# Regrouping the first tiles of a pruned matrix product: tiles 3 to 6 in one group of rows, one transposing load per tile

## The chip, the cores and the metric

The kernel runs on one core of a Trainium2 chip. The metric is the device time of one execution in microseconds (us), the median over several runs. The core has a matrix engine (PE, with its weight loads shown apart as PEld), a vector engine (DVE), a scalar engine (ACT), GpSimd (POOL) and a sync engine (SP). SP and ACT also issue transfers here: each has a queue in which its instructions are taken strictly in order, and the transfers of both run on the same 16 DMA engines.

## The reference

```python
B, S, D = 16, 512, 1024
wg = w.reshape(G, M, D)                       # M = 4 neighbouring rows of w
mag = jnp.abs(wg)
order = jnp.argsort(mag, 1)
thr = jnp.take_along_axis(mag, order[:, M - N:M - N + 1, :], 1)   # N = 2
mask = (mag >= thr).astype(w.dtype)
wp = (wg * mask).reshape(D, D)                # the two largest of four are kept
return jnp.einsum("bsd,df->bsf", x, wp) + b
```

The input x has 8192 rows (tokens) of K = 1024 numbers, w is 1024 by 1024, everything is bfloat16.

## The kernel before

**Tiles.** The 8192 rows are 64 tiles of 128 rows. PE contracts over partitions, so a tile of x must stand in SBUF with K on the partitions: transposed. For most tiles the load itself transposes (`dma_start_transpose`). The kernel takes the two halves of K apart at the start: the "upper" half is K 0 to 511 (`HK` = 512, g = 0), the "lower" half K 512 to 1023 (g = 1).

**The first seven tiles.** Pruning w takes DVE and ACT some 25 us, piece by piece (six pieces; four of the upper half of K with 256 columns each, two of the lower with 512). So that PE can begin early, the upper halves of tiles 0 to 6 (`NPK` = 7) are loaded untransposed (`load_x`), transposed by PE itself (tokens `T`, line 195), copied out by ACT (`C`), and multiplied with each piece as soon as it is pruned (`M`, line 216). Their sums over the upper half are copied to SBUF by ACT (`S`, `U`). Pruned pieces are also spread to another layout, `wp_nat`, by plain transfers (tokens `W`: `W0.0` and `W0.1` for the two column halves of the upper K, `W1.0`, in the parts p on SP and q on ACT, and `W1.1` for the lower K); every spread issues one transfer for each of four blocks of 128 rows of K, and each matmul of line 244 reads one such block.

**Groups.** A transposing load is done for the lower halves of tiles 0 to 5 (`load_low`, tokens `Y`), and `GROUPS` says which rows a tile means there: within a group of n tiles, row n*p + t of the group is row p of its tile t (`tokens`, line 93). Input and output use the same view, so the tiles of a group interleave their rows. Before, the groups are tiles 0 to 2, 3 to 5 and 6 alone. One transposing load takes a whole group of 384 rows, and the weight loads of a tile read every third column of it. Tile 6 (`SOLO`), alone in its group, has its lower half in the transposing load of tiles 7 to 11 (`load_lead`, 5 "lead" tiles): `X0` loads the upper halves of tiles 7 to 11 (640 rows), `X1` the lower halves of 6 to 11 (768 rows).

**Closing.** Tiles 7 to 11 get their upper half on PE (tokens `E` and `A`) while the lower half of w is still being pruned. Then 24 closes follow (line 416), one for each of the tiles 0 to 11 and column half: four matmuls over the lower half of K with `wp_nat`'s last four blocks, and an eviction by DVE that adds the bias or the stored upper sum. Their order is (8,0) (9,0) (10,0) (11,0) (7,0) (6,0) (3,0) (4,0) (5,0), the same nine with column half 1, and then (2,0) (2,1) (0,0) (0,1) (1,0) (1,1). After them come batches of 4 and six times 8 tiles, 16 matmuls a tile, from transposing loads of whole rows (`load_batch`, tile xb, two buffers). `outp` has ten output buffers, `psum_o` six banks.

**Order.** The order on PE, DVE, ACT and SP is written out by hand in the strings of `order` (line 268); SP's is:

```python
        "sp": (
            "W0.0 Z W0.1 X1 W1.0p Y1 Y0 W1.1"
        ),
```

In front of it SP issues part of the loads of w and x and then X0; behind it the first two xb. `Z` loads the last columns of w and the bias. PE's string begins "T5a T3a T4a T6a M5.0t M3.0t". The order of a queue's instructions is also the order in which they wait: what stands behind a waiting instruction waits with it.

Of the kernel before, what the change touches and what calls it, by code (L numbers as in the profile page):

```python
# [10 lines left out]
def kernel(  # L11
# [7 lines left out]
    nc = tc.nc  # L19
    P = 128  # L20
    bf16 = mybir.dt.bfloat16
# [7 lines left out]
    KT = D // P  # L29
# [3 lines left out]
    FH = 512  # L33
    CW = 256
    HK = D // G
    assert G == 2 and Dout == 2 * FH and HK == 512
    xf = x.flatten_outer_dims()
    of = out.flatten_outer_dims()

    NPK = 7  # L40
    LEAD = 5
    STG = 8
    SOLO = 6
    GROUPS = ((0, 3), (3, 6), (6, 7))
    LATE = 6
    sizes = (4, 8, 8, 8, 8, 8, 8)
    batches = []
    t0 = NPK + LEAD
# [5 lines left out]
    const = ctx.enter_context(tc.tile_pool(name="const", bufs=1))  # L54
# [11 lines left out]
    def seq(eng, inst):  # L66
        if eng in tails:
            tc.add_manual_dep(inst.ins, tails[eng].ins.name, NOSYNC, reason="program order")
        tails[eng] = inst
        return inst  # L70

    def pe(i):
        return seq("pe", i)
# [7 lines left out]
    def sp(i):  # L81
        return seq("sp", i)
# [10 lines left out]
    def tokens(dram, t):  # L93
        a, b_ = next(s for s in GROUPS if s[0] <= t < s[1])
        return dram[a * P:b_ * P].rearrange("(p t) k -> p t k", p=P), t - a
# [13 lines left out]
        for t in range(ta, tb):  # L109
            x_sb[t] = xs[:, t - ta, :]  # L110

    xlead = const.tile([P, KT, (LEAD + 1) * P], bf16)

    def load_lead(g):
        t0 = NPK - g
        sp(nc.sync.dma_start_transpose(out=xlead[:, 4 * g:4 * g + 4, (t0 - SOLO) * P:],
                                       in_=xf[t0 * P:(NPK + LEAD) * P, g * HK:(g + 1) * HK]))
        return {t: xlead[:, :, (t - SOLO) * P:(t - SOLO + 1) * P] for t in range(t0, NPK + LEAD)}

    xnat, held = {}, {}  # L120

# [10 lines left out]
    load_w(0, 768, 1024)  # L132
    load_w(1, 0, 512)
    xnat.update(load_lead(0))
    pieces = [(0, 0, 256), (0, 256, 512), (0, 512, 768), (0, 768, 1024), (1, 0, 512), (1, 512, 1024)]

# [95 lines left out]
                                start=(new and m == ms.start), stop=(left[key] == 0),  # L232
                                skip_group_check=True))

    def load_low(u):
        a, b_ = GROUPS[u]
        xlow = const.tile([P, 4, (b_ - a) * P], bf16, name=f"xlow{u}")
        sp(nc.sync.dma_start_transpose(out=xlow[:], in_=xf[a * P:b_ * P, HK:]))
        xq = xlow[:].rearrange("p k (q t) -> p k q t", t=b_ - a)
        return {a + t: xq[:, :, :, t] for t in range(b_ - a)}  # L240

    def nat(xt, ps, c0, c1, k0=0, k1=KT, first=0, last=KT - 1, koff=0):
        for kt in range(k0, k1):
            pe(nc.tensor.matmul(ps, lhsT=xt[:, kt - koff, :], rhs=wp_nat[:, kt, c0:c1],  # L244
                                start=(kt == first), stop=(kt == last)))
# [15 lines left out]
    def stage(key):  # L261
        solo = key[1] == "h"
        q, h, at = (pair_of[key[0]], key[2], int(key[0] != SOLO)) if solo else (key[0], key[1] // 2, key[1] % 2)
        if (q, h) not in staged:
# [21 lines left out]
            "S3b3 S2b3 U7h0 W1.0q U7h1"  # L286
        ),
        "sp": (
            "W0.0 Z W0.1 X1 W1.0p Y1 Y0 W1.1"
        ),  # L290
    }
    written = {"X0"}
    p = {}
# [53 lines left out]
    def emit(eng, tok):  # L347
# [10 lines left out]
        elif tok[0] == "Z":  # L358
            load_w(1, 512, 1024)
            sp(nc.sync.dma_start(bias_sb[:], b.partition_broadcast(P)))  # L360
        elif tok[0] == "X":
            xnat.update(load_lead(int(tok[1:])))
        elif tok[0] == "Y":
            xnat.update(load_low(int(tok[1:])))
        elif tok[0] == "E":
            open_solo(int(tok[1:]))
        elif tok[0] == "U":
            t, h = map(int, tok[1:].split("h"))
            stage((t, "h", h))
        elif tok[0] == "A":  # L370
            open_nat(*map(int, tok[1:].split("h")))
        elif tok[0] == "C":
            copy_xt(int(tok[1:-1]))
        elif tok[0] == "M":
            mm_piece(*map(int, base[1:].split(".")), part[k])
        elif tok[0] == "S":
            stage(tuple(map(int, tok[1:].split("b"))))
        else:
            i = int(base[-1])
            if i not in p:  # L380
                p[i] = Piece(i)
            if eng == "act":
                p[i].abs_act()
            else:
                p[i].do(base[:-1], part[k], half.get(k, slice(0, 2)))
# [42 lines left out]
    def evac(o, ps, c0, c1, add=None):  # L428
        if add is None:
            dve(nc.vector.tensor_tensor(o[:, c0:c1], ps, bias_sb[:, c0:c1], op=Alu.add))  # L430
        else:
            dve(nc.vector.tensor_tensor(o[:, c0:c1].rearrange("p (n c) -> p n c", n=2),  # L432
                                        ps.rearrange("p (n c) -> p n c", n=2), add, op=Alu.add))
# [7 lines left out]
    def store(eng, t, o, c0=0, c1=Dout):  # L441
        issue(eng, rows(t)[:, c0:c1], o[:, c0:c1])
# [4 lines left out]
    def close(t, h):  # L447
        if t not in outs:
            outs[t] = outp.tile([P, Dout], bf16, name="o")
        ps = held.pop((t, h), None)  # L450
        if ps is None:
            ps = psum_o.tile([P, FH], fp32, name="ps")
        nat(xnat[t], ps[:], h * FH, (h + 1) * FH, 4, 8, first=4 if t < STG else 0, koff=4 if t < SOLO else 0)
        add = None
        if t < STG:
            st, at = staged[(pair_of[t], h)], pairs[pair_of[t]].index(t)
            add = st[:, at, :, :] if SOLO in pairs[pair_of[t]] else st[:, :, at, :]
        evac(outs[t], ps[:], h * FH, (h + 1) * FH, add)
        closed[t] = closed.get(t, 0) + 1
        if closed[t] == 2:  # L460
            store("act", t, outs.pop(t))

    for t, h in closes:
        close(t, h)
# [3 lines left out]
    for bi, (tb, nb) in enumerate(batches):  # L468
        if bi:
            load_batch(bi + 1)  # L470
        for j in range(nb):
            t = tb + j
            xt = xnat[t]
            o = outp.tile([P, Dout], bf16, name="o")
            if t == NT - 1:
                for n, (c0, c1) in enumerate(((0, FH), (FH, FH + CW), (FH + CW, Dout - P), (Dout - P, Dout))):
                    ps = psum_o.tile([P, FH], fp32, name="ps")
# [44 lines left out]
```

## Time and profile before

| | us |
|---|---|
| median of 3 runs | 233.0 |
| lowest, highest | 232.53, 233.31 |
| the profiled execution, its own time | 233.15 |
| its span, first to last instruction | 231.3 |
| PE busy | 227.1 (98%) |
| PE weight loads busy | 110.5 (48%) |
| DVE busy | 107.8 (47%) |

The views read below are rows of one profiled execution. A row of a timeline has start, length, engine, line, operation, what it writes and reads, how many instructions are merged, and in brackets the idle time before it and what ended it. SPq and ACTq are the queues' own instructions, such as the issuing of a transfer; a transfer lands some time after its issue. A row of a tile's view has the shortest, median and longest duration in ns, and the first and last start in us.

### The profile page before, as it was taken

The page shows a single profiled execution, that of the slowest core. Times are in us where ns is not written, and L with a number is a line of the kernel's source. Part 1 is how long each engine was busy: PE and PEld are TensorE (multiplying, and loading weights), DVE is VectorE, ACT ScalarE, POOL GpSimd, SP SyncE. Part 2 cuts the span into 40 slices and gives each one's busy share as a digit, 9 for nine tenths or more (in the row PEclk, how much of TensorE's full clock was granted, in tenths as well). Part 3 has the DMA queues.
Part 4 walks back from the last instruction along what each step waited for, and adds up shares of the span by engine and source line. Part 5 has one row for each costly group of instructions (what it writes and reads, how often), then busy time and mean ns, then how long its engine had stood idle before and what let it go on. Part 6 is the DMA issues. An engine that isn't in the chain of part 4 may idle for free.

```text
span 231.3 us, 2831 instructions
## 1 busy us (share of the span) xinstructions
PE 227.1 (98%) x1144; PEld 110.5 (48%) x1144; DVE 107.8 (47%) x196; ACT 14.0 (6%) x27; POOL 17.6 (8%) x15
## 2 busy tenths in 40 slices
PE   8899999999999999999999999999999999999995
PEld 4886444444444444444444444444444444444443
DVE  3999878844324324424424424424423423433434
ACT  3784100000000000000000000000000000000000
POOL 1000199700000000000000000000000000000000
PEclk9999999999999999999999999999999999999999
DMA  6999989998699222991249821796128942122122
GB/s 200 270 206 252 231 176 223 230 296 241 224 197 300 92 94 66 260 263 53 86 116 252 221 91 67 146 254 196 69 91 204 238 148 84 55 91 91 50 89 91
DMA packets 79292, 38.19 MB, mean 165 GB/s; under 512 B 64176, under 2 KB 71728, under 8 KB 79280
## 3 DMA queue, kind: packets, MB, share of 16 engines
q1 hardware_dynamic: 68352, 20.75, 44.3%
q10 hardware_dynamic: 10928, 17.27, 21.4%
q8 instruction: 9, 0.15, 0.3%
q14 instruction: 3, 0.02, 0.1%
HBM read 3.28 MB, written 16.78 MB: 87 GB/s over the span
## 4 chain that ended last, share of the span: by engine, by line
PE 96%; DMA 2%; ACTq 0%; DVE 0%; issue 0%
PE ps L244 88%; PE ps L230 5%; PE tp L244 2%; DMA x<-in_x_dram 2%; ACTq L100 0%; PE ps L200 0%; PE tp L200 0%; DVE o L430 0%
## 5 line engine op out<-in xcount | busy, mean ns | idle before, releaser
L244 PE MATMUL ps<-wp_nat,xb 128*128 128x512 bf16 (+2 forms) x848 | 179.8, 375 | 0.0
L244 PEld LDWEIGHTS <-xb 128*128 128x128 bf16 x848 | 82.4, 98 | 97.5
L430 DVE TENSOR_TENSOR o<-ps,bias_sb 128x512 bf16<-128x512 f32 (+1 forms) x112 | 71.6, 677 | 113.0 <-PE ps L244 112.9
L426 POOL TENSOR_TENSOR st<-st,bias_sb 128x1024 f32<-128x1024 f32 x8 | 16.7, 2125 | 0.0
L244 PE MATMUL ps<-wp_nat,xlead 128*128 128x512 bf16 x64 | 14.8, 379 | 0.0
L244 PEld LDWEIGHTS <-xlead 128*128 128x128 bf16 x88 | 8.6, 98 | 10.2
L230 PE MATMUL ps<-wp,xt 128*128 128x256 bf16 x112 | 12.9, 273 | 0.0
L432 DVE TENSOR_TENSOR o<-ps,st 128x512 bf16<-128x512 f32 x16 | 11.0, 691 | 3.6 <-PE ps L244 2.0
L230 PEld LDWEIGHTS <-xt 128*128 128x128 bf16 x112 | 10.7, 98 | 1.2
L244 PE MATMUL ps<-wp_nat,xlow 128*128 128x512 bf16 x48 | 10.7, 379 | 0.0
L266 ACT COPY st<-ps 128x512 f32<-128x512 f32 x14 | 7.4, 595 | 3.4 <-PE ps L230 3.3
L244 PEld LDWEIGHTS <-xlow 128*128 128x128 bf16 x48 | 5.0, 103 | 5.4
L164 DVE TENSOR_TENSOR mag<-mag,hi 128x256 bf16<-128x256 bf16 (+2 forms) x15 | 6.2, 439 | 0.2
L164 DVE TENSOR_TENSOR wp<-w_sb,mag 128x256 bf16<-128x256 bf16 (+2 forms) x15 | 6.1, 436 | 0.1
L244 PE MATMUL tp<-wp_nat,xlead 128*128 128x512 bf16 x24 | 6.0, 379 | 0.0
L143 PE MATMUL ps<-const-bfloat16-1.0 128*128 128x128 bf16 (+1 forms) x20 | 3.9, 380 | 0.8 <-PEq L506 0.8
L174 DVE TENSOR_SCALAR mag<-w_sb 128x512 uint16<-128x512 uint16 (+2 forms) x5 | 2.3, 477 | 3.5 <-DMA w_sb<-in_w_dram 3.5
L143 PEld LDWEIGHTS <-const-bfloat16-1.0 128*128 128x128 bf16 x20 | 2.1, 135 | 2.4 <-issue 2.4
L164 DVE TENSOR_TENSOR hi<-mag 128x512 bf16<-128x512 bf16 (+2 forms) x7 | 3.2, 459 | 0.1
L164 DVE TENSOR_TENSOR lo<-mag 128x512 bf16<-128x512 bf16 (+1 forms) x6 | 3.1, 509 | 0.0
L200 PEld LDWEIGHTS <-x 128*128 128x128 bf16 x28 | 1.9, 115 | 1.3 <-DMA x<-in_x_dram 1.2
L415 POOL COPY pruned<-wp 128x1 bf16<-128x1 bf16 x1 | 0.2, 187 | 26.8 <-DVE wp L164 26.8
(18 smaller groups left out, 18.1 us busy)
## 6 DMA issues: line engine op xcount, KB each, us to landing
out_dram<-o ACTq DMA_DIRECT2D x58, 256.0 KB, 2.4
wp_nat<-wp SPq DMA_DIRECT2D x14, 128.0 KB, 3.6
out_dram<-o ACTq DMA_DIRECT2D x10, 128.0 KB, 1.7
w_sb<-in_w_dram SPq DMA_DIRECT2D x2, 512.0 KB, 5.6
w_sb<-in_w_dram SPq DMA_DIRECT2D x3, 256.0 KB, 5.4
x<-in_x_dram SPq DMA_DIRECT2D x2, 256.0 KB, 4.5
x<-in_x_dram ACTq DMA_DIRECT2D x2, 128.0 KB, 4.1
bias_sb<-in_b_dram SPq DMA_DIRECT2D x1, 256.0 KB, 4.8
```

The source lines that it names most:

```text
L143: pe(nc.tensor.matmul(warm_ps[:, :rep * P], lhsT=nc.const_aps.tensor(1.0, [P, P], bf16), rhs=nc.const_aps.tensor(1.0, [P, rep * P], bf16), ...
L164: dve(nc.vector.tensor_tensor(out, a, b_, op=op))
L174: dve(nc.vector.tensor_single_scalar(self.mag[:, ms, :].bitcast(u16), self.w[:, ms, :].bitcast(u16), 0x7FFF, op=Alu.bitwise_and))
L200: pe(nc.tensor.transpose(tp[:, m, :], xg[:, m, :], ident[:]))
L230: pe(nc.tensor.matmul(ps[:, c0 + d:c1 + d], lhsT=xpk[t][:, m, :], rhs=wp[:, g, m, c0:c1], start=(new and m == ms.start), stop=(left[key] = ...
L244: pe(nc.tensor.matmul(ps, lhsT=xt[:, kt - koff, :], rhs=wp_nat[:, kt, c0:c1], start=(kt == first), stop=(kt == last)))
L266: act(nc.scalar.copy(staged[(q, h)][:, at, :, :].rearrange("p t c -> p (t c)"), ps_open.pop(key)[:]))
L415: pool(nc.gpsimd.tensor_copy(out=pruned[:], in_=wp[:, 1, 3, Dout - 1:]))
L426: pool(nc.gpsimd.tensor_tensor(st[:], st[:], bias.to_broadcast([P, 2, 2, CW]), op=Alu.add))
L430: dve(nc.vector.tensor_tensor(o[:, c0:c1], ps, bias_sb[:, c0:c1], op=Alu.add))
L432: dve(nc.vector.tensor_tensor(o[:, c0:c1].rearrange("p (n c) -> p n c", n=2), ps.rearrange("p (n c) -> p n c", n=2), add, op=Alu.add))
```

## The change

Tile 6 joins the group of tiles 3 to 5, which has four tiles then, so that row 4p + t of the group is row p of tile 3 + t; tiles 0 to 2 stay as they are. X1 loads tiles 7 to 11 alone, like X0. Each of the tiles 0 to 6 gets a transposing load of its own for its lower half: 128 rows, which lie three rows apart in the first group and four in the second. On SP's queue Y6, Y3, Y4 and Y5 come ahead of W1.1, and Y2, Y0 and Y1 behind it.

```diff
-    GROUPS = ((0, 3), (3, 6), (6, 7))
+    GROUPS = ((0, 3), (3, 7))
...
-    xlead = const.tile([P, KT, (LEAD + 1) * P], bf16)
+    xlead = const.tile([P, KT, LEAD * P], bf16)
 
     def load_lead(g):
-        t0 = NPK - g
-        sp(nc.sync.dma_start_transpose(out=xlead[:, 4 * g:4 * g + 4, (t0 - SOLO) * P:],
-                                       in_=xf[t0 * P:(NPK + LEAD) * P, g * HK:(g + 1) * HK]))
-        return {t: xlead[:, :, (t - SOLO) * P:(t - SOLO + 1) * P] for t in range(t0, NPK + LEAD)}
+        sp(nc.sync.dma_start_transpose(out=xlead[:, 4 * g:4 * g + 4, :],
+                                       in_=xf[NPK * P:(NPK + LEAD) * P, g * HK:(g + 1) * HK]))
+        return {t: xlead[:, :, (t - NPK) * P:(t - NPK + 1) * P] for t in range(NPK, NPK + LEAD)}
...
-    def load_low(u):
-        a, b_ = GROUPS[u]
-        xlow = const.tile([P, 4, (b_ - a) * P], bf16, name=f"xlow{u}")
-        sp(nc.sync.dma_start_transpose(out=xlow[:], in_=xf[a * P:b_ * P, HK:]))
-        xq = xlow[:].rearrange("p k (q t) -> p k q t", t=b_ - a)
-        return {a + t: xq[:, :, :, t] for t in range(b_ - a)}
+    def load_low(t):
+        xlow = const.tile([P, 4, P], bf16, name=f"xlow{t}")
+        xv, n = tokens(xf, t)
+        sp(nc.sync.dma_start_transpose(out=xlow[:], in_=xv[:, n, HK:]))
+        return {t: xlow}
...
-            "W0.0 Z W0.1 X1 W1.0p Y1 Y0 W1.1"
+            "W0.0 Z W0.1 X1 W1.0p Y6 Y3 Y4 Y5 W1.1 Y2 Y0 Y1"
...
-        nat(xnat[t], ps[:], h * FH, (h + 1) * FH, 4, 8, first=4 if t < STG else 0, koff=4 if t < SOLO else 0)
+        nat(xnat[t], ps[:], h * FH, (h + 1) * FH, 4, 8, first=4 if t < STG else 0, koff=4 if t < NPK else 0)
```

## The prediction

> **What bounds the kernel now.** I read the page first, then PE's busy time by stretches, the chain of work that ended last, and the timelines of PE, DVE and SP's queue around the lines that change. The page and the stretches:
>
> ```profile
> PE 227.1 (98%) x1144; PEld 110.5 (48%) x1144; DVE 107.8 (47%) x196; ACT 14.0 (6%) x27; POOL 17.6 (8%) x15
> ...
> PE 96%; DMA 2%; ACTq 0%; DVE 0%; issue 0%
> ```
>
> ```profile
> 6.37:28.34 21.97, 21.97 (x169) 1.00 1.05 236
> 28.34:48.70 20.36, 20.36 (x96) 1.00 1.07 227
> 48.70:228.70 180.00, 179.97 (x850) 1.00 0.57 149
> ```
>
> Columns: stretch, length, PE busy (instructions), granted clock, DMA share, GB/s. From 6.37 us to 228.70 us PE never stops, at full clock. The change removes no matmul, so after 6.37 there is nothing to win. Time can be won only before 6.37, and lost wherever something new makes PE wait. The chain shows what sets 6.37, and PE's timeline the gap (the bracket is idle time before the row):
>
> ```profile
> 1.78 4.54 DMA x<-in_x_dram
> 6.33 0.05 issue
> 6.37 0.41 PE ps L200 x4
> 6.79 1.31 PE ps L230 x12
> ```
>
> ```profile
> 5.36 0.39 PE L200 MATMUL ps<-ident,x 128*128 128x128 bf16 x4
> 6.37 0.41 PE L200 MATMUL ps<-ident,x 128*128 128x128 bf16 x4 [0.63 <-DMA x<-in_x_dram]
> 6.62 1.47 PE L230 MATMUL ps<-wp,xt 128*128 128x256 bf16 x12
> ```
>
> The load issued at 1.78 is the second x load on ACT's queue, load_x(SOLO, SOLO + 1): the upper half of tile 6. T6a waits for it, and the first real matmul (M5.0t) stands behind T6a.
>
> The other limits are SP's queue and, from 19 to 49 us, the DMA engines, whose share is over 1 in the stretches above.
>
> ```profile
> 5.71 5.87 SPq L116 DMA_TRANSPOSE xlead<-in_x_dram  x1
> ...
> 19.80 3.45 SPq L116 DMA_TRANSPOSE xlead<-in_x_dram  x1
> 23.35 1.81 SPq L100 DMA_DIRECT2D wp_nat<-wp  x2
> 25.21 3.83 SPq L238 DMA_TRANSPOSE xlow<-in_x_dram  x2
> ```
>
> ```profile
> 29.13 3.45 SPq L100 DMA_DIRECT2D wp_nat<-wp  x4
> 32.63 4.07 SPq L404 DMA_TRANSPOSE xb<-in_x_dram  x1
> ```
>
> In order: X0; X1; W1.0p; Y1 and Y0; W1.1; the first xb.
>
> **The change, part by part.**
>
> *Tile 6's upper half and the loads beside it.* Same bytes and same 1 KB runs; the rows read for tile 6 lie 8 KB apart, not 2 KB, those of tiles 3 to 5 8 KB, not 6 KB. The trace has 8 KB steps: the first two loads of w take two rows of 512 bytes out of every 8 KB. The first two rows here are those loads; the other two are all five x loads, and the two of ACT's queue.
>
> ```profile
> w_sb<-in_w_dram SPq DMA_DIRECT2D x1, 128.0 KB, 2.8
> ...
> w_sb<-in_w_dram ACTq DMA_DIRECT2D x1, 128.0 KB, 3.0
> ```
>
> ```profile
> DMA to landing us min/median/max: 3.6/4.5/5.2
> ```
>
> ```profile
> DMA to landing us min/median/max: 3.6/4.1/4.5
> ```
>
> With 8 KB steps 128 KB landed in 2.8 and 3.0 us, so the step itself does not look dear. Tile 6's 4.54 is the slower of the two ACT loads, though it is as large as the other. Bounds for tile 6's load: 3.6 (the fastest x load) and 5.2 (the slowest). A faster landing is not all gain, since M5.0t needs the first product of DVE:
>
> ```profile
> 5.97 0.49 DVE L164 TENSOR_TENSOR wp<-w_sb,mag 128x256 bf16<-128x256 bf16 x2
> ```
>
> The first of these two products takes some 0.28 us (284 ns, as the shortest of their kind), so M5.0t cannot start before about 6.25 + 0.05 = 6.30 against 6.62. The gain is at most 0.32 us; the loss at 5.2 us is 0.66. I take 0.2 of gain: the new load moves as much as the ACT load that landed in 3.6, so it is likelier nearer to that one than above 4.54.
>
> *X1 shrinks from 768 rows to 640.* 3.45 us over 768 rows is 4.5 ns a row, so 2.88 us: X1's issue ends at 22.68, not 23.25. W1.0p needs the product that ends at 21.23 + 1.23 = 22.46, so it starts at 22.72, 0.63 earlier:
>
> ```profile
> 21.23 1.23 DVE L164 TENSOR_TENSOR wp<-w_sb,mag 128x2048 bf16<-128x2048 bf16 x1
> ...
> 26.81 1.22 DVE L164 TENSOR_TENSOR wp<-w_sb,mag 128x2048 bf16<-128x2048 bf16 x1
> ```
>
> PE waits for none of it now, so the worth is 0. It is cover: the last spread of W1.0p is issued at 24.4 and lands at 28.1 (the rows below), and the second matmul of the first close needs it at 28.18 + 0.22 = 28.40. The cover grows from 0.3 to about 0.9, less what the front gains.
>
> ```profile
> L100 SPq DMA_DIRECT2D wp_nat<-wp x1: 800/800/800, 24.4 to 24.4; - x1
> ...
> DMA to landing us min/median/max: 3.7/3.7/3.7
> ```
>
> ```profile
> 28.18 2.75 PE L244 MATMUL ps<-wp_nat,xlead 128*128 128x512 bf16 x12
> ```
>
> *Two loads of 384 rows become seven of 128, in two groups.* Price of one, first by the two loads of before:
>
> ```profile
> L244 PEld LDWEIGHTS <-xlow x48: 102/103/104, 33.1 to 48.5; 128*128 128x128 bf16 x48
> ...
> L238 SPq DMA_TRANSPOSE xlow<-in_x_dram x2: 1421/1892/2362, 25.2 to 26.7; - x2
> ...
> DMA to landing us min/median/max: 4.6/5.3/6.0
> ```
>
> A third of each is 0.47 and 0.79 us. X0's 5.87 us over 640 rows (9.2 ns a row, in the crowd of the first loads) would make 1.17. A fixed price per load is bounded below by nothing; above, I let a small load cost all that a large one does, 2.36. Value: a third of 1.89, 0.63, and 0.04 between two, 0.67 each, as the first xb (512 rows of twice the width in 4.07 us, 3.98 ns per row of 512) shows no fixed part: larger loads are not cheaper by the row than 1421 ns over 384 rows (3.7).
>
> W1.0p ends at 22.72 + 1.81 = 24.53; Y6, Y3, Y4 and Y5 take 4 x 0.67 = 2.68 and end at 27.25. W1.1 then waits for its product, 26.81 + 1.22 = 28.03, and starts at 28.09 instead of 29.13: 1.04 earlier. At 1.17 it starts at 24.57 + 4.84 = 29.41, 0.28 later; at 2.36, at 34.17, 5.04 later. Who waits: the first close with the upper columns, whose last matmul needs W1.1's last spread:
>
> ```profile
> L100 SPq DMA_DIRECT2D wp_nat<-wp x1: 603/603/603, 32.0 to 32.0; - x1
> ...
> DMA to landing us min/median/max: 3.1/3.1/3.1
> ```
>
> ```profile
> 35.95 2.75 PE L244 MATMUL ps<-wp_nat,xlead 128*128 128x512 bf16 x12
> ```
>
> It lands at 32.0 + 3.1 = 35.1; PE wants it between 35.95 (if the close waits for all four) and 36.60. So W1.1 may come 0.9 us later for nothing, and comes 1.04 earlier: 0. The lower halves are wanted later still: closes follow each other by 4 x 0.216 = 0.864 us from 28.18, so tiles 6, 3, 4, 5 at 32.5, 33.4, 34.2 and 35.1, tile 2 at 43.7. With 6.0 us from issue to landing Y6 is there at 30.6 and Y5 at 32.6 (34.2 at 1.17 each). None waits.
>
> *W1.1 moves ahead of Y2, Y0, Y1, and these ahead of the first xb.* W1.1's 3.45 end at 31.54, three loads at 0.67 end at 33.6: the first xb starts at 33.6 instead of 32.63, 1.0 later (3.9 at 1.17 each). The first and the second xb before:
>
> ```profile
> L404 SPq DMA_TRANSPOSE xb<-in_x_dram x1: 4072/4072/4072, 32.6 to 32.6; - x1
> ...
> DMA to landing us min/median/max: 6.4/6.4/6.4
> ```
>
> ```profile
> L404 SPq DMA_TRANSPOSE xb<-in_x_dram x1: 15961/15961/15961, 36.7 to 36.7; - x1
> ...
> DMA to landing us min/median/max: 18.0/18.0/18.0
> ```
>
> The first would land 6.4 us after issue at 40.0, at the worst 42.9; tile 12 wants it at 48.7. The second landed at 54.7; 3.9 later is 58.6, and tile 16 wants it at 48.9 + 4 x 3.45 = 62.7. Cost 0 by both bounds. Stores share the DMA engines with it and free DVE's output buffers; DVE waited once:
>
> ```profile
> 48.90 4.48 PE L244 MATMUL ps<-wp_nat,xb 128*128 128x512 bf16 x20
> 49.23 1.29 DVE L432 TENSOR_TENSOR o<-ps,st 128x512 bf16<-128x512 f32 x2 [1.09 <-DMA out_dram<-o]
> ```
>
> Behind that eviction PE has six banks: it stalls only when tile 14 begins, at 48.9 + 2 x 3.45 = 55.8. Stores can be 5 us later than now and cost nothing.
>
> *Weight loads of xlow.* Columns with a step of three become contiguous. The loads took 102 to 104 ns (above), against 97 or 98 from xlead, under matmuls that start 216 ns apart (20 of them in 4.48 us, the last one 379 ns long): 0 either way.
>
> ```profile
> L244 PEld LDWEIGHTS <-xlead x88: 97/98/98, 19.4 to 40.7; 128*128 128x128 bf16 x88
> ```
>
> Sum against the profiled execution's own time, 233.15 (span 231.3, 1.85 around it): 233.15 - 0.2 + 0 + 0 + 0 + 0 = 232.95. It stands 0.15 above the median of 233.0; I forecast 232.9.
>
> The Trainium skill speaks against the split: "DMA: Bandwidth & Descriptors", section "Rules for kernel authors", tells to coalesce many small transfers, as under 64 KB mostly overhead is paid, and to make one at least 1 MiB; its "Latency and other measured facts" has a fixed cost of some 2 us. Paid in turn on the queue, these 2 us would make W1.1 about 3.5 us late and the sum some 236, by that page an estimate. The rows show the fixed part as latency that overlaps: four spreads were issued in 3.45 us though each landed 3 us and more after its issue.
>
> **The rivals.** (1) *Slower: a small transposing load has a fixed price, and W1.1 comes late.* It decides from (29.13 + 0.9 - 24.57) / 4 = 1.37 us for each of the four loads. At 2.36 W1.1 is 5.04 late, less 0.9 to 1.54 of cover: 3.5 to 4.1 of stall, 236.5 to 237; at 1.9 about 235. For it: one 384-row load did take 2.36. Against: the other took 1.42 for the same work, so 2.36 was crowd, not a fixed price. (2) *Slower: tile 6's load lands later*, at 5.2 us, as 8 KB steps over one stretch shared by four tiles: 0.66 more, 233.8; from 0.7 on it can be measured. Against: the w loads above. (3) *Faster: in executions not shown PE stalls at 28.40 or 35.95*, where covers are 0.3 and 0.9, and the change widens both. With the full 0.32 of the front, 232.2. Against: the profiled execution, slower than the median, shows no such stall. (4) *Later xb loads push the stores until DVE and then PE wait*: decides from 5 us, 234. (5) *It wins nothing at all*, tile 6 landing as before: 233.1, within the forecast.
>
> **How the numbers follow.** Forecast, with (5): 0.62. (1) 0.09, (2) 0.14, (3) 0.12, (4) 0.03. A measurement of this kernel tells about 0.3% (0.7 us) from no change. Faster is (3) and the luck of the forecast's lower end: 0.13; slower (1), (2) and (4), less the part of (2) under 0.7: 0.25; same 0.62. The range reaches from (3) to a little above (2): 232.2 to 234.1; the forecast's own is 232.5 to 233.5.
>
> **What would show it.** Right: T6a starts at 6.1 to 6.4 in PE's timeline, PE busy without a gap from there, W1.1's issue at about 28.1, each Y under 0.9 us, the first xb at 33 to 35. Wrong: a wait of PE for DMA at tile 6 longer than 0.63, or for wp_nat near 36 us; or a gain over 0.7 us, for which the trace of before has no place.

## The result and the profile after

| | before | changed |
|---|---|---|
| median of 20 runs, us | 232.94 | 233.35 |
| lowest, highest | 232.53, 233.54 | 232.86, 234.24 |
| the profiled execution, its span | 233.15, 231.3 | 233.39, 231.6 |

The ratio is 1.0017, with a 95% interval of 1.0009 to 1.0025: 0.41 us slower by the medians. That is less than 0.3%, but the 20 runs a side resolve it, and a small gain had been forecast. A few executions of the runs below, at a lower granted clock, took 237 us or more; the ratios and intervals leave them out, the medians do not.

The stretches of PE in the changed kernel, with the columns of before:

```profile
6.37:28.34 21.97, 21.95 (x170) 1.00 1.00 236
28.34:48.70 20.36, 20.36 (x96) 1.00 0.91 198
48.70:228.70 180.00, 180.00 (x850) 1.00 0.61 153
```

In this execution PE is still all but without a gap from its first real matmuls to its end. The whole difference of the two profiles, 0.27 us of span, must lie at the two ends. Start of the PE timeline and the landings of ACT's two x loads, changed kernel:

```profile
5.05 1.04 PE L199 MATMUL tp<-ident,x 128*128 128x128 bf16 x8
5.89 0.75 PE L199 MATMUL ps<-ident,x 128*128 128x128 bf16 x8
6.48 0.69 PE L229 MATMUL ps<-wp,xt 128*128 128x256 bf16 x3
```

```profile
DMA to landing us min/median/max: 3.7/4.1/4.4
```

Tile 6's half lands 0.17 us sooner, at 6.16, and M5.0t starts at 6.48 instead of 6.62. Yet nothing of it is left later: the first eight transposes took 1.04 us against 0.64, the copies of ACT came later, and a weight load waited 0.2 us for one. The last matmul starts at 228.50, before at 228.45.

What SP did in between, changed kernel; then the issues of its seven loads, and the first xb:

```profile
24.34 5.39 SPq L237 DMA_TRANSPOSE xlow<-in_x_dram  x4
29.83 2.83 SPq L100 DMA_DIRECT2D wp_nat<-wp  x4
32.71 3.92 SPq L237 DMA_TRANSPOSE xlow<-in_x_dram  x3
36.67 4.87 SPq L402 DMA_TRANSPOSE xb<-in_x_dram  x1
```

```profile
L237 SPq DMA_TRANSPOSE xlow<-in_x_dram x7: 1264/1265/1463, 24.3 to 35.4; - x7
```

```profile
L402 SPq DMA_TRANSPOSE xb<-in_x_dram x1: 4867/4867/4867, 36.7 to 36.7; - x1
...
DMA to landing us min/median/max: 10.7/10.7/10.7
```

A load of 128 rows costs SP 1.26 us, the first of the seven 1.46; before, the first of the two, of 384 rows, took 1.42. W1.1 starts 0.7 us later than before, the first xb 4.0 us later. It also takes 10.7 us to land, not 6.4, and is there at 47.4; tile 12 wants it at 48.9.

The other end is the last store and SP's closing instructions, which wait for the DMA semaphores. The rows are the last store, its landing, and SP's instructions from 230.5 to 231.0 us; before:

```profile
L100 ACTq DMA_DIRECT2D out_dram<-o x1: 338/338/338, 229.0 to 229.0; - x1
...
DMA to landing us min/median/max: 1.5/1.5/1.5
```

```profile
L517 SPq EVENT_SEMAPHORE  x2: 17/22/28, 230.5 to 230.8; - x2
```

and after:

```profile
L100 ACTq DMA_DIRECT2D out_dram<-o x1: 339/339/339, 229.1 to 229.1; - x1
...
DMA to landing us min/median/max: 1.5/1.5/1.5
```

```profile
L515 SPq EVENT_SEMAPHORE  x4: 28/28/28, 230.6 to 230.8; - x4
```

The trace's issue records show that transfers take eight semaphores in turn, and that SP waits for these at the end in five waits of a fixed order, one behind the other; where nothing holds them they start 0.063 us apart. Before, the last store had the eighth semaphore, that of the last wait: when it landed at 230.50 this one wait was left (the second row counted there is a later barrier). Five more transfers move the last store on by five, to one of the second wait: when it lands at 230.58, that wait and three more are still to be taken, though all their transfers have landed. From the last landing to the end of the span it is 0.83 us before and 1.02 us after.

### The profile page after: what moved, and what is told of

Its sections match the earlier page's. It is cut to its first block, busy times and chain, and to the rows that moved or that the text cites. A ratio compares the mean times of both kernels' runs of the same rounds, so it can differ in the third digit from the quotient of the medians.

```text
span 231.6 us, 2836 instructions
## 1 busy us (share of the span) xinstructions
PE 227.9 (98%) x1144; PEld 110.9 (48%) x1144; DVE 107.9 (47%) x196; ACT 14.0 (6%) x27; POOL 17.6 (8%) x15
## 4 chain that ended last, share of the span: by engine, by line
PE 97%; DMA 2%; ACTq 0%; DVE 0%; issue 0%
PE ps L242 88%; PE ps L229 5%; PE tp L242 2%; DMA x<-in_x_dram 2%; PE tp L199 1%; PE ps L199 0%; ACTq L100 0%; DVE o L428 0%
## 5 line engine op out<-in xcount | busy, mean ns | idle before, releaser
L242 PE MATMUL ps<-wp_nat,xlead 128*128 128x512 bf16 x56 | 13.1, 379 | 0.0
L242 PE MATMUL ps<-wp_nat,xlow 128*128 128x512 bf16 x56 | 12.4, 379 | 0.0
L242 PEld LDWEIGHTS <-xlead 128*128 128x128 bf16 x80 | 7.8, 98 | 9.3
L229 PEld LDWEIGHTS <-xt 128*128 128x128 bf16 x112 | 10.7, 98 | 1.4 <-ACT xt L204 0.2
L242 PEld LDWEIGHTS <-xlow 128*128 128x128 bf16 x56 | 5.5, 98 | 6.6
L199 PEld LDWEIGHTS <-x 128*128 128x128 bf16 x28 | 2.4, 127 | 0.4 <-DMA x<-in_x_dram 0.3
```

The costliest lines, as they stand in the source:

```text
L199: pe(nc.tensor.transpose(tp[:, m, :], xg[:, m, :], ident[:]))
L229: pe(nc.tensor.matmul(ps[:, c0 + d:c1 + d], lhsT=xpk[t][:, m, :], rhs=wp[:, g, m, c0:c1], start=(new and m == ms.start), stop=(left[key] = ...
```

## The experiments

The first four were to separate the two ends and the two halves of the change, groups and loads.

**e1.** In the changed kernel:

```diff
-    LATE = 6
+    LATE = 9
```

> The changed kernel with the last nine tiles stored in halves instead of six: three more stores, so that the last store falls on the eighth of the eight DMA semaphores again (in the changed kernel it falls on the fifth in the order in which SP's closing instructions wait; before, on the last). Theory 'the tail': the changed kernel pays three closing waits of 0.065 us each after its last landing, so this one is 0.2 us faster than the changed kernel, about 233.15, and one closing wait is left after the last landing. Rival 'the loads': the closing waits do not count and the whole 0.41 us comes from the early part; then it stays at 233.3 to 233.4.

**e2.** In the kernel before:

```diff
-    LATE = 6
+    LATE = 3
```

> The kernel before with the last three tiles stored in halves instead of six: three stores fewer, so that the last store falls on the same semaphore as in the changed kernel. Nothing else of the change is in it. Theory 'the tail': 0.2 us slower than before, ratio about 1.0008, with three closing waits after the last landing. Rival 'the loads': same as before, ratio 1.0000.

**e3.** The changed kernel with the loads of before:

```diff
-            "W0.0 Z W0.1 X1 W1.0p Y6 Y3 Y4 Y5 W1.1 Y2 Y0 Y1"
+            "W0.0 Z W0.1 X1 W1.0p Y1 Y0 W1.1"
...
+        a, b_ = GROUPS[u]
+        sp(nc.sync.dma_start_transpose(out=xlow[:], in_=xf[a * P:b_ * P, HK:]))
```

> The changed kernel's grouping (tiles 3 to 6 in one group) with one transposing load for a whole group, 512 and 384 rows, in the old order: as many transfers as before, so the last store's semaphore is that of before. Theory 'the tail plus the front': the other half of the 0.41 us comes from the x loads of tiles 3 to 6, whose rows lie 8 KB apart now, so this one is 0.2 us slower than before, ratio about 1.0009, with PE's first real matmul late. Rival 'split loads': the grouping costs nothing and it equals before, 1.0000.

**e4.** The changed kernel with the groups of before:

```diff
-    GROUPS = ((0, 3), (3, 7))
+    GROUPS = ((0, 3), (3, 6), (6, 7))
```

> The changed kernel with the old groups (0 to 2, 3 to 5, 6): one transposing load of 128 rows per tile, five transfers more than before, the last store on the changed kernel's semaphore; x loads as before. Theory 'the tail plus the front': 0.2 us slower than before, ratio about 1.0008, all of it in the closing waits. Rival 'split loads': 0.4 us slower, as much as the changed kernel, 1.0017.

Measured, beside 233.00 for the kernel before on the same chip:

| | median, us | ratio, 95% interval | closing waits from the last landing on | last landing to end of span, us |
|---|---|---|---|---|
| e1 | 233.05 | 1.0002, 0.9988 to 1.0016 | 1 | 0.83 |
| e2 | 233.21 | 1.0001, 0.9989 to 1.0014 | 4 | 1.03 |
| e3 | 232.95 | 0.9996, 0.9984 to 1.0008 | 1 | 0.83 |
| e4 | 233.88 | 1.0025, 1.0005 to 1.0045 | 4 | 1.03 |

The ratio is not the quotient of the two medians (for e2 that would be 1.0009); where they differ, the interval says what is known. The last two columns are from the profiles. Here is SP in the same stretch of time, first in e2, which has nothing of the change but the semaphore, then in e1:

```profile
L517 SPq EVENT_SEMAPHORE  x4: 28/28/28, 230.6 to 230.7; - x4
```

```profile
L515 SPq EVENT_SEMAPHORE  x1: 28/28/28, 230.8 to 230.8; - x1
```

The closing waits came and went with the count of the transfers alone, and carry 0.2 us. The times do not speak against it, but their intervals are too wide to show it by themselves. e3 says that the grouping costs nothing: my half-theory of dear x loads fell. e4 was slower than expected, which I took to point at the loads; its profile does not show that, as PE's one wait there is for tile 6's upper half, which landed at 6.77.

**f1, f2.** The changed kernel and e1 once more, side by side.

> The changed kernel once more, beside the next one on the same chip. Theory 'the tail': about 0.2 us over before and over the next kernel; theory 'tail plus early stalls': 0.4 us over before, some runs over 234.

> The changed kernel with the last nine tiles stored in halves, once more: what is left of the difference when the closing waits are taken out. Theory 'the tail': it equals before within 0.1 us. Theory 'tail plus early stalls': it stays 0.2 us over before, with single runs far above, since the first xb lands only 1.5 to 3.5 us ahead of its need in the changed kernel.

f1: 233.42, 1.0017 (1.0006 to 1.0029). f2: 233.04, 1.0007 (0.9997 to 1.0018), the kernel before 232.94. The difference of the changed kernel is real; with the closing waits out, 0.1 us or so stays, which the interval cannot tell from nothing.

**f3.** In the changed kernel:

```diff
-            "W0.0 Z W0.1 X1 W1.0p Y6 Y3 Y4 Y5 W1.1 Y2 Y0 Y1"
+            "W0.0 Z W0.1 X1 W1.0p Y6 Y3 Y4 Y5 Y2 Y0 Y1 W1.1"
```

> The changed kernel with all seven lower-half loads ahead of W1.1 on SP's queue. In the profile of the changed kernel one load of 128 rows takes SP 1.26 to 1.46 us, so W1.1 is issued 3.9 us later, at about 33.7, and its last spread lands at about 39.2, while PE wants it between 36.0 and 36.65. Theory 'fixed price per load': PE waits 2.6 to 3.2 us for wp_nat at the first close of the upper columns, time 235.9 to 236.6. Rival 'a load costs by its rows', as the prediction had it (0.63 us): W1.1 is issued 1.9 us later and PE waits at most 0.9 us, time about 234.

Measured 237.83, 1.0190 (1.0155 to 1.0224), above both. SP's queue, PE's timeline, and the stretches (stretch, length, busy PE, PEld, DVE, ACT and POOL, granted clock, DMA share, GB/s):

```profile
23.86 10.20 SPq L237 DMA_TRANSPOSE xlow<-in_x_dram  x7
34.17 2.48 SPq L100 DMA_DIRECT2D wp_nat<-wp  x4
```

```profile
36.86 0.38 PE L242 MATMUL ps<-wp_nat,xlead 128*128 128x512 bf16 x1 [0.86 <-DMA wp_nat<-wp]
37.67 0.74 PE L242 MATMUL ps<-wp_nat,xlead 128*128 128x512 bf16 x2 [0.43 <-DMA wp_nat<-wp]
39.18 3.52 PE L242 MATMUL ps<-wp_nat,xlead 128*128 128x512 bf16 x9 [0.77 <-DMA wp_nat<-wp]
```

```profile
36.00:39.60 3.60, 1.54 (x5) 0.48 (x5) 0.70 (x2) 0.00 (x0) 3.60 (x3) 1.00 0.95 213
39.60:43.10 3.50, 3.50 (x10) 1.31 (x9) 1.74 (x3) 0.00 (x0) 3.50 (x3) 0.52 1.22 306
```

A price per load it is: seven loads took 10.2 us. PE waited for the spreads one by one, 2.06 us in three waits. And the time rose by more than the waits: behind them the granted clock was 0.52 for 3.5 us. From the first matmul of tile 7 to that of tile 12 it is 33.74 us here and 29.36 in the first profile of the changed kernel, 4.4 us more.

**f4.** In the kernel before, tile 6's transposes moved back on PE:

```diff
-            "T5a T3a T4a T6a M5.0t M3.0t M4.0t M5.0s
+            "T5a T3a T4a M5.0t M3.0t M4.0t T6a M5.0s
```

> The kernel before with T6a behind M5.0t M3.0t M4.0t in PE's order: tile 6's load no longer stands between PE and its first real matmul. Theory 'the front follows tile 6's load': M5.0t starts at about 6.3 us whatever that load does (6.62 in the profile of before), PE ends 0.1 to 0.3 us earlier, ratio 0.9987 to 0.9996. Rival 'the front is set by the product of DVE and by the granted clock': no difference, 1.0000.

A miss: 233.41, 1.0018 (1.0010 to 1.0026), slower. Part of the PE timeline and of the list of waits up to 8 us:

```profile
6.30 0.49 PE L230 MATMUL ps<-wp,xt 128*128 128x256 bf16 x3 [0.38 <-DVE wp L164]
6.63 0.39 PE L200 MATMUL ps<-ident,x 128*128 128x128 bf16 x4
```

```profile
PEld L230 <- ACT xt L205: 0.9, 3, 0.4
```

M5.0t did start at 6.30, as soon as DVE's product was there. But M6.0t needs ACT's copy of tile 6's transposes, and these were later now; PE lost there what it had won, and more: the first matmul of tile 7 starts at 19.75, before at 19.54.

**g1 to g4.** g1 is e4 and g2 the kernel before, both with `LATE = 9`. g3 moves the first xb in the changed kernel, also with `LATE = 9`: `B` is a new token for `load_batch(0)`, in place of the call behind the queues.

```diff
-            "W0.0 Z W0.1 X1 W1.0p Y6 Y3 Y4 Y5 W1.1 Y2 Y0 Y1"
+            "W0.0 Z W0.1 X1 W1.0p Y6 Y3 Y4 Y5 W1.1 B Y2 Y0 Y1"
```

g4 is e3 with other groups and `LATE = 4`:

```diff
-    GROUPS = ((0, 3), (3, 7))
+    GROUPS = ((0, 2), (2, 3), (3, 5), (5, 7))
...
-            "W0.0 Z W0.1 X1 W1.0p Y1 Y0 W1.1"
+            "W0.0 Z W0.1 X1 W1.0p Y3 Y2 W1.1 Y1 Y0"
```

> The kernel with one load per tile and the old groups, its last nine tiles stored in halves, so that the closing waits are those of before. Without that its median was 0.9 us over before, with runs up to 238. Theory 'tail plus early stalls': 0.1 to 0.6 us over before and again single runs of 237 or more. Theory 'the tail': equal to before within 0.1 us.

> The kernel before with the last nine tiles stored in halves: three stores more, so that the last store falls on the semaphore that SP's closing instructions wait for first. Theory 'the tail': four closing waits after the last landing, 0.26 to 0.3 us over before, and 3.13 to 3.17 us from the last matmul's start to the end of the span (2.88 in before, 3.10 in the changed kernel). Rival 'storing in halves itself saves time': less than 0.2 us over before.

> The changed kernel with the first xb ahead of Y2 Y0 Y1 on SP's queue and the last nine tiles stored in halves. The first xb is issued at about 33, not 36.7, and lands at about 39 to 40, 9 us ahead of its need instead of 1.5. Theory 'early stalls, by the late xb': it equals before, no run over 234.5. Rival 'nothing of it is the xb': 0.1 us over before like the changed kernel with the closing waits taken out, with single runs far above.

> Groups 0 and 1, 2, 3 and 4, 5 and 6; one transposing load per group (256, 128, 256, 256 rows), the two of tiles 3 to 6 ahead of W1.1, the last four tiles stored in halves so that the closing waits are those of before. Theory 'a price per load': 256 rows take SP 1.3 to 1.5 us, hardly more than 128; W1.1 is issued as soon as its product is there, at about 28.1, and the first xb at about 35. Rival 'a price by rows': 256 rows take 2.4 to 2.6 us. In both PE has no wait, and the time is that of before within 0.1 us.

| | median, us (before 233.12) | ratio, 95% interval |
|---|---|---|
| g1 | 233.39 | 1.0014, 0.9992 to 1.0037 |
| g2 | 233.19 | 1.0006, 0.9996 to 1.0015 |
| g3 | 232.87 | 0.9992, 0.9982 to 1.0003 |
| g4 | 233.71 | 1.0037, 1.0018 to 1.0056 |

g1's profile has the first stall of PE on the xb. The waits of PE:

```profile
PE ps L242 <- DMA xb<-in_x_dram: 0.4, 1, 0.4
```

g2 has 1.07 us from the last landing to the end, five closing waits, and an interval that takes in both readings; the median, 0.07 us over before, is nearer to the rival, so it is not excluded that storing in halves itself saves a little in e1, f2, g3 and h2. From its last matmul, which starts at 228.17, to the end it is 3.11 us, a little under the expected 3.13. g3, with the first xb early, is level with before. g4 shows loads of 128 and 256 rows in one kernel:

```profile
L237 SPq DMA_TRANSPOSE xlow<-in_x_dram x4: 1290/1404/1547, 24.8 to 33.2; - x4
```

One of 256 rows costs 1.3 to 1.55 us. Compared in the same place, as the first of these loads on the queue, the price is nearly the same from 128 rows (1.29 to 1.56 us over all profiles) to 384 (1.40 to 1.60). It is not so everywhere: 384 rows in the second place took 1.82 to 2.46, and the 512 rows of e3 took 2.96 in the first. But g4 is 0.6 us slower, which neither theory had: the x load of tiles 3 and 4, which are neighbouring rows here, lands at 6.09 (4.80 to 5.34 in all other profiles), and T3a waits for it. That the rows are the reason is not shown, by one profile.

```profile
6.13 0.41 PE L199 MATMUL tp<-ident,x 128*128 128x128 bf16 x4 [0.85 <-DMA x<-in_x_dram]
```

**h1 to h3.** h1 is g3 with `LATE = 6`, that is the changed kernel with the first xb moved and nothing else; h2 is g3 again; h3 is the changed kernel.

> The changed kernel with the first xb ahead of Y2 Y0 Y1 on SP's queue and nothing else: the closing waits stay. Theory 'closing waits and late xb': 0.2 us over before (ratio 1.0005 to 1.0011), 0.2 us under the changed kernel, no run over 234.5. Rival 'the xb counts for nothing': 0.4 us over before, as the changed kernel.

> The same with the last nine tiles stored in halves, which takes the closing waits out; once more. Theory 'closing waits and late xb': equal to before within 0.1 us (ratio 0.9996 to 1.0004), or a little under it. Rival 'the xb counts for nothing': 0.1 to 0.2 us over before.

> The changed kernel beside them: 0.4 us over before, ratio 1.0013 to 1.0021, by both theories.

h1: 233.16, 1.0003 (0.9991 to 1.0016). h2: 232.99, 0.9995 (0.9985 to 1.0004). h3: 233.39, 1.0011 (0.9999 to 1.0023). The kernel before: 233.13. By medians the late xb is worth 0.23 us and the closing waits 0.17. The profiled execution of h3 took 234.46, and shows the changed kernel itself stalling; SP's queue, the first xb, and PE:

```profile
24.32 6.92 SPq L237 DMA_TRANSPOSE xlow<-in_x_dram  x4
31.34 2.49 SPq L100 DMA_DIRECT2D wp_nat<-wp  x4
33.87 3.92 SPq L237 DMA_TRANSPOSE xlow<-in_x_dram  x3
37.83 16.85 SPq L402 DMA_TRANSPOSE xb<-in_x_dram  x2
```

```profile
L402 SPq DMA_TRANSPOSE xb<-in_x_dram x1: 6210/6210/6210, 37.8 to 37.8; - x1
...
DMA to landing us min/median/max: 12.1/12.1/12.1
```

```profile
50.00 4.28 PE L242 MATMUL ps<-wp_nat,xb 128*128 128x512 bf16 x19 [1.14 <-DMA xb<-in_x_dram]
```

Four loads of 128 rows took 6.92 us here, 1.5 more than in the first profile, as the fourth alone took 2.70 (why, no run shows); the xb was issued at 37.83 and landed at 50.0, and tile 12 began 1.14 us late. h1 moved the xb only:

```profile
33.74 4.09 SPq L260 DMA_TRANSPOSE xb<-in_x_dram  x1
37.88 4.05 SPq L237 DMA_TRANSPOSE xlow<-in_x_dram  x3
```

```profile
DMA to landing us min/median/max: 6.2/6.2/6.2
```

Here it lands at 39.9, before at 39.1. Why it takes 6 us in one place and 11 to 12 in the other is seen on ACT's queue in the first profile of the changed kernel: the stores begin at 37.8, and share the engines with an xb that is issued from 36.67 on. In the kernel before, and in h1, its issue ends about there.

```profile
37.78 5.03 ACTq L100 DMA_DIRECT2D out_dram<-o  x6
```

The DMA queues bear it out. Queue q1 has SP's transfers, q10 ACT's; a row has packets, MB and the share of the 16 engines. From the issue to the landing of the first xb, before (32.63 to 39.07) and changed (36.67 to 47.4):

```profile
q1 hardware_dynamic: 4922, 1.44, 104.0%
```

```profile
q1 hardware_dynamic: 5018, 1.27, 66.0%
q10 hardware_dynamic: 768, 1.41, 38.5%
```

The profiles can also be cut into parts, at the first matmul of tile 7 (E0), the first of tile 12 (the first to read an xb), and the last matmul of all:

| us | E0 starts | from there to tile 12 | to the last matmul | to the end |
|---|---|---|---|---|
| before | 19.54 | 29.36 | 179.55 | 2.88 |
| changed | 19.59 | 29.36 | 179.55 | 3.10 |
| f1 | 19.55 | 29.36 | 179.56 | 3.10 |
| h3 | 19.34 | 30.66 | 179.57 | 3.10 |
| e1 | 19.85 | 29.35 | 179.56 | 2.86 |
| f2 | 19.71 | 29.35 | 179.56 | 2.87 |
| g1 | 19.76 | 29.89 | 179.57 | 2.87 |
| h1 | 19.36 | 29.35 | 179.56 | 3.11 |

The last matmuls take the same time everywhere, and the part up to tile 12 differs only where PE stalls (in no other profile by more than 0.1 us). What is left is the end, the stall, and the front, that is all ahead of E0, which starts anywhere from 19.2 to 20.0 over all profiles. Leaving out f3, where PE itself came late, seven profiles have the first xb behind seven single loads and W1.1 (those of the changed kernel, of e1, e4, f1, f2, g1 and h3): it landed 0.04 to 4.2 us ahead of tile 12, and in h3 and g1 PE stalled for it. In the three with the xb moved (g3, h1, h2) it landed 7.6 us ahead or more.

## Why the prediction was wrong

- **What bounds the kernel: half right, and here the sum failed.** PE is gapless once it has begun, and the loss is where PE waits; but "lost wherever something new makes PE wait" left out the end. The sum took what lies behind the last matmul as fixed, and had no term for it. It is not fixed: five more transfers turn the last store to another semaphore and add three closing waits, 0.2 us. That is half of the result, and by itself more than the 0.1 us of gain that was forecast.
- **Tile 6's load: not settled, and what looks right is luck.** 0.2 us of gain was chosen. In the three profiles of the changed kernel M5.0t starts at 6.48, 6.38 and 6.42 (before: 6.62). But with the same loads tile 6's half landed at 6.64 in e1, and with those of before at 5.42 in g2, so neither the sign nor the size is shown. Little of it is left at E0, either: 19.59, 19.55 and 19.34, against 19.54 before and 19.26 in g2. The bound of 0.32 looked at DVE's product only, not at ACT's copies and the speed of the transposes ahead of them.
- **The price of a small load: mis-sized by two.** 0.63 us was taken, 1.26 measured (in four of the profiles one load took 1.71 to 2.70). The inference from xb, that no fixed part shows, failed: as the first of these loads on the queue 128 rows cost as much as 384. W1.1 came 0.7 us later instead of 1.04 earlier. The first rival had the right mechanism, and a measured price just below the 1.37 us from which it was to decide. In h3 the mean of four was above it and W1.1 came 2.2 us later; even there PE did not wait, as each matmul waits for its own spread only and W1.1 took 2.49 us, not 3.45. f3 shows what it costs beyond the cover. The Trainium skill, "DMA: Bandwidth & Descriptors", section "Rules for kernel authors", spoke against the split and was right in direction; the runs show a price of about 1.3 us per issue on the queue.
- **The later xb: the landing that was furthest off.** "Cost 0 by both bounds" put it at 42.9 us at the worst, with 6.4 us from issue to landing as before. It landed at 47.4 and, in another execution, at 50.0: issued 4 to 5 us later, it met the stores. The fourth rival had later xb loads, but looked for the harm in the stores and DVE's buffers, not in the xb itself.
- **The last step of the sum.** 232.95 less the 0.15 by which the profiled execution stands above the median is 232.8, not the 232.9 that was forecast. The measured 233.35 lies inside the forecast's own 232.5 to 233.5; what was missed is the direction.
- **Cover of W1.0, weight loads of xlow: right.** No wait on either; the third rival's gain did not show.

What is shown: the closing waits, in every profile, by the semaphore alone; and that the changed kernel stalls on the late xb in some executions, one of three profiled. That the xb makes up the other 0.2 us of the median is not shown. For it: ahead of E0 the changed kernel runs the same instructions as e3, which is level with before, so behind E0 only a stall can cost it more than the closing waits; an estimate from the seven profiles with the late xb, (1.30 + 0.53) / 7, is 0.26 us an execution; and h1, h2 and g3, with the xb moved, have lower medians than h3, e1 and f2. Against it: the profiled executions of the changed kernel that lie near the median, 233.39 and 233.35 us, have no stall, and the intervals of h1 and h3 overlap. The lowest end of the interval of the result, 0.21 us, is about what the closing waits alone would give, so a part of the 0.41 may be chance of the front. None of the versions beats the kernel before by more than its interval: the best, the early xb with the closing waits out, has 0.9992 (0.9982 to 1.0003) and 0.9995 (0.9985 to 1.0004).

## What to carry to other kernels

Splitting one transfer into several on one queue is to be costed by a price per issue, and everything behind it on that queue has to be followed to its landing, with the transfers that it will meet there, not with the latency that it had in its old place. A kernel that is bound from its first to its last matmul still has two ends: count what stands between the last landing and the end, and ask whether the number of transfers changes it. A load whose cover has shrunk from 9.8 us to 1.5 looks harmless in one profile and stalls in the next.

## What was not expected of the hardware

- The issue of a transposing load took SP 1.26 us at best for 128 rows of 512 numbers, 1.3 to 1.55 for 256, 1.40 to 2.46 for 384 and 2.96 for 512.
- In f3 three waits of PE of 0.86, 0.43 and 0.77 us within 3 us were followed by a granted clock of 0.52 for 3.5 us, so the stall cost 4.4 us, over twice the 2.06 of these waits. One wait of 1.14 us in h3 was not followed by a lower clock. The Trainium skill, "TensorE: Matmul & The Clock Gate", section "What's actually happening", has the clock halved after an idle window of some 3.4 us; the row of f3 shows it after waits of 2.06 us in all, none longer than 0.86.
- The first transposes of PE took 0.64 us for eight in one execution and 1.04 in another, with the same instructions ahead of them: in the first they start 0.056 us apart, in the second 0.107. The same section of the Trainium skill says that the window runs freely and does not start with the kernel, so that the switch to full speed comes at another place each time; the two rows agree.
- The x load of tiles 3 and 4, as neighbouring rows, landed so late in g4 that T3a waited 0.85 us; in the other profiles, where these rows stand in groups of three or four, T3a had no wait of its own.
